# First layer's weight sums converted where they are made, a new product order, other places for raw tokens, and a planner with a DMA queue

## The chip, the cores and the metric

One Trainium2 chip, one of its cores. The metric is device microseconds of one execution, the median of the runs shown. Lower is better.

## The reference

Sigmoid attention for 4 batches of 12 heads, 448 tokens of 64 numbers each, then two feed-forward layers over all 1792 tokens (768 to 2048 to 768):

```python
scores = q @ k.T / sqrt(64) - log(448)          # per batch and head
x = (1 / (1 + exp(-scores))) @ v                # reshaped to 1792 x 768
r = maximum(x @ w_in1, 0);  g = s * r * r + b;  x = g @ w_out1
h = x @ w_in2;  g = maximum(h, 0) + alpha * minimum(h, 0);  y = g @ w_out2
```

The four weight arrays arrive as 64-bit floats; all else is 32-bit.

## The kernel before, in words

**Precision and products.** Each 32-bit operand is split into a high part (a cast on ScalarE) and the rest (a subtraction on VectorE), both in the matmul's fast 32-bit format. `split` does this. A product is then three matmuls (lines 406 to 408): high by low, high by high, low by high. On top of that every layer's matrix product uses one level of a seven-product block scheme, so that a 2 by 2 block product needs the products M1 to M7 instead of eight; the left factors are the weight blocks and their sums (`LEFT`), the right factors are token blocks and their differences.

**Phases.** The tokens are two groups of two batches (g = 0, 1). After attention come eight phases in this order: (layer 0, g 0) in and out, (layer 0, g 1) in and out, then the same two for layer 1. They are numbered 0 to 7 here: even ones are in phases (x times w_in, and the nonlinearity), odd ones out phases (times w_out). Every phase has 504 matmuls of 128 x 128 by 448 columns. An in phase loops over eight block rows (`mp`), each with the seven products in `IN_ORDER` and three 128-deep steps: 63 matmuls. An out phase goes through the seven products in `OUT_ORDER`, each with three block rows of eight steps.

**Weights: quads and units.** `quad` prepares one block row of weights, a "quad" in the code's name. It loads two rows of 64-bit weights into `R64[0]` and `R64[1]`, turns them into 32-bit numbers (line 263 on ScalarE into `CVA`, lines 266 and 271 on VectorE into `QUAD`), makes the four block sums (line 284 on VectorE), and stores the seven blocks to an array in DRAM (`w32`, line 302). A quad has eight VectorE operations. There are 34 quads: 8 for each w_in, 9 for each w_out (three chunks of columns, by three block rows). `QUAD`, `CVA` and `R64` are single, so one quad follows another: the next may write `QUAD` only when the store of the one before has landed. Matmuls get weights by `unit`: it loads 1024 columns from DRAM into one of two `RAW` buffers and splits them into one of three `RING` buffers, 21 units in each phase.

**Tokens.** Seven right factors, the planes `X`, stand in a field of 37 slots (`SLOTS`). `make_x` makes them from four raw token blocks `XRAW` by splits and differences (line 335). For g 0 of layer 0 the raw blocks come straight out of attention, in the memory of the ring. For the other three (layer, group) pairs they are in DRAM, and `load_x` loads them in the out phase before, in its last product, into `XRAW[1]`. This buffer lies on the same memory as `R64`, `CVA` and part of `QUAD` (`PROD`, 5376 columns from its start).

**Order.** Nothing is issued in program order. Every operation is handed to `Plan.add` with an engine, a duration, and the 64-column memory cells that it reads and writes; what touches the same cells keeps program order. `Plan.order` then simulates the engines: at each step it takes the operation that can start first, and among equals the one with the earliest due time; TensorE keeps program order. The due times come from TensorE's ideal times. DMAs are all issued from SyncE's queue, in the order planned; in the plan each holds the queue for its whole transfer. On the chip every engine's operations run in that fixed order and wait for semaphores. `produce(n)` puts the next n quads into the program: 20 during attention (8 w_in1, 9 w_out1, 3 w_in2), 9 after phase 1, 5 after phase 3.

Of the kernel before, what the change touches and what calls it, by code (L numbers as in the profile page):

```python
# [18 lines left out]
CELL = 64  # L19

IN_ORDER = ["M1", "M5", "M6", "M2", "M7", "M4", "M3"]
# [5 lines left out]
class Plan:  # L29
# [25 lines left out]
    def order(self):  # L55
# [5 lines left out]
        ideal, t = {}, 0.0  # L61
        for i, op in enumerate(self.ops):
            if op[0] == "PE":
                ideal[i] = t
                t += op[1]
        late = [0.0] * n
        for i in range(n - 1, -1, -1):
            eng, dur, lat = self.ops[i][:3]
            x = min((late[s] for s in succ[i]), default=t + 50) - dur - lat
            late[i] = min(x, ideal[i]) if i in ideal else x  # L70
        left = [len(op[3]) for op in self.ops]
        est = [0.0] * n
        pe = [i for i in range(n) if i in ideal]
# [5 lines left out]
        free = {}  # L79
        done = []  # L80
        while len(done) < n:
            best = None
            for eng, cand in open_.items():
                if not cand:
                    continue
                f = free.get(eng, 0.0)
                if eng == "PE":
                    i = pe[pe_at]
                    if i not in cand:
                        continue  # L90
                    pick = (max(f, est[i]), late[i], i)
                else:
                    pick = min((max(f, est[i]), late[i], i) for i in cand)
# [7 lines left out]
            end = start + dur  # L101
            free[eng] = end
            done.append(i)
            for s in succ[i]:
                est[s] = max(est[s], end + lat)
# [3 lines left out]
        return done  # L109
# [26 lines left out]
def tile_kernel(  # L136
# [59 lines left out]
    RAW = [own(f"raw{i}", UNIT) for i in range(NRAW)]  # L196
    TMP = [own(f"tmp{i}", S) for i in range(NTMP)]
    NEG = own("neg", 2 * S)
# [7 lines left out]
    def act_t(n, psum=False):  # L206
        return (0.15 if psum else 0.19) + 0.834e-3 * n

    def dve_t(n, psum=False):
        return 0.155 + (1.06e-3 if psum else 1.04e-3) * n  # L210
# [4 lines left out]
    def dma_t(n):  # L215
        return 0.1 + n * 4 * P / 330e3
# [3 lines left out]
    MM = 0.2005  # L220
# [11 lines left out]

    w64 = {(0, "in"): w_in1, (0, "out"): w_out1, (1, "in"): w_in2, (1, "out"): w_out2}
    w32 = {k: drp.tile([P, 7 * NMP * WQ], F32, name=f"w{k[0]}{k[1]}") for k in w64}

    def quad(m, kind, k, c):

        order = IN_ORDER if kind == "in" else OUT_ORDER
# [8 lines left out]
        for row in range(2):  # L247
# [9 lines left out]
            x, y = ("A11", "A12") if row == 0 else ("S3", "A22")  # L257
# [18 lines left out]
            add("ACT", act_t(2 * n), f0, cv, ca)  # L276
# [11 lines left out]
        tt("S1", "S3", "A22", ALU.add)  # L288
        tt("S3", "A11", "S3", ALU.subtract)
# [16 lines left out]
    n_unit = [0]  # L306
    ring = {}

    def unit(m, kind, i):
        g = n_unit[0]  # L310
        n_unit[0] += 1
        raw, dst = RAW[g % NRAW], RING[g % NRING]
        load(
            sb(raw, UNIT), w32[m, kind][:, i * UNIT : (i + 1) * UNIT], UNIT,
            [("d", m, kind, 8 * i + j) for j in range(8)], cells(raw, UNIT),
        )
        split(dst, dst + UNIT, raw, UNIT)
        ring[m, kind, i] = dst
# [27 lines left out]
    X = [[slots(f"xo{p}{i}", p, 3 * i, 3) for i in range(7)] for p in range(2)]  # L346
# [17 lines left out]
    def make_x(par, raw):  # L364
        p = [XRAW[raw] + i * XB for i in range(4)]
        pl = X[par]

        def half(i, src):
            split(pl[i], pl[i] + XB, src, XB)

        half(0, p[0])
        minus(p[0], p[1], p[0], XB)
        half(1, p[0])
        minus(p[0], p[3], p[0], XB)
        half(2, p[0])
        half(3, p[2])
        minus(p[1], p[3], p[1], XB)
        half(4, p[1])
        minus(p[0], p[0], p[2], XB)
        half(5, p[0])  # L380
        half(6, p[3])

    def load_x(m, g):
        for i in (0, 1, 3, 2):
            to = XRAW[1] + i * XB
            load(
                sb(to, XB), x_dram[m, g][:, i * XB : (i + 1) * XB], XB,
                [("x", m, g, i, j) for j in range(KH)], cells(to, XB),
            )
# [51 lines left out]
    def nonlinear(m, par, mp, ps_):  # L441
# [4 lines left out]
        if m == 0:  # L446
# [5 lines left out]
                "ACT", act_t(n) + 0.15,  # L452
# [4 lines left out]
        for row in range(2):  # L457
            some = [p for p in ps_ if p // 2 == row]
            if not some:
# [12 lines left out]
                "DVE", dve_t(n),  # L472
# [6 lines left out]
    def in_phase(m, par):  # L479
        NU = 7 * NMP * KH // 8  # L480
        made = 0
        for mp in range(NMP):
# [3 lines left out]
            second = {"M2", "M4", "M7"}  # L486
            for i, x in enumerate(IN_ORDER):
                terms = []
                for kc in range(KH):
                    g = (mp * 7 + i) * KH + kc  # L490
                    while made <= g // 8:
                        unit(m, "in", made)
                        made += 1
                    w = ring[m, "in", g // 8] + (g % 8) * P
                    xo = X[par][i]
                    terms.append((w, w + UNIT, xo + kc * S, xo + XB + kc * S))
# [18 lines left out]
                elif x == "M4":  # L515
# [3 lines left out]
                else:  # L519
# [20 lines left out]
    def out_phase(m, g, par, middle):  # L540
# [19 lines left out]
        for i, x in enumerate(OUT_ORDER):  # L560
# [4 lines left out]
            for k in range(NDP):  # L565
                unit(m, "out", i * NDP + k)
                w = ring[m, "out", i * NDP + k]
                for (j0, j1), o in zip(CHUNKS, GB[par][i % 2]):
                    terms = [
                        (w + j * P, w + (UNIT + j * P), o + (j - j0) * S, o + (j1 - j0 + j - j0) * S)  # L570
# [79 lines left out]
    def qk(u):  # L650
# [17 lines left out]
        add("PE", 0.81, f, r, pcells(k), PE_LAT)  # L668
# [13 lines left out]
    def av(u):  # L682
# [23 lines left out]
        add("PE", 0.81, f, r + w, w, PE_LAT)  # L706

    def take_x(q):
# [4 lines left out]
        t = XRAW[0] + o if bb < 2 else tmp()  # L713
# [37 lines left out]
    quads = []  # L751
    for m in range(2):
        quads += [(m, "in", k, 0) for k in range(NMP)]
# [92 lines left out]
```

## Time and profile before

| | |
|---|---|
| median of 3 runs | 1026.64 us (1022.49, 1026.64, 1033.18) |
| the profiled execution's own time | 1022.74 us |
| its span, first to last instruction | 1020.9 us |
| mean granted TensorE clock | 0.980 |
| busy: TensorE, weight loads | 972.0 us (95%), 828.7 us (81%) |
| busy: VectorE, ScalarE | 762.6 us (75%), 625.8 us (61%) |
| moved by DMA | 222.68 MB, 218 GB/s over the span |

The span is what the trace covers. The execution's own time is 1.8 us longer, and the median of the runs 3.9 us longer than that. Busy times count an engine's operations; TensorE's matmuls overlap in the pipeline.

### The profile page before, as it was taken

The numbers are of one execution on the slowest core, as the hardware profiler recorded it, in microseconds if no ns is written. First come the engines' busy times: TensorE is split into PE (matmuls) and PEld (weight loads), VectorE is DVE, ScalarE is ACT, GpSimd is POOL, SyncE is SP. The second block draws the span as 40 slices with busy tenths as digits, with TensorE's granted clock in tenths as the row PEclk, the third lists the DMA queues.
The fourth block names the chain that finished last, engine by engine and source line by source line (L and its number), as shares of the span: only waits on it lengthen the run. The fifth ranks groups of instructions, "written<-read, shape, count | busy, mean of one in ns | idle before, by whom it ended". The sixth has DMA issues, their size and how long they took to land.

```text
span 1020.9 us, 13856 instructions
## 1 busy us (share of the span) xinstructions
PE 972.0 (95%) x5424; PEld 828.7 (81%) x5424; DVE 762.6 (75%) x896; ACT 625.8 (61%) x675; POOL 0.2 (0%) x4
## 2 busy tenths in 40 slices
PE   9999999998699979999999889998999999999998
PEld 5533368987598968999899769997999999999997
DVE  2476467679996867668999589868997856679872
ACT  7889856877553536778665246656645455576440
POOL 0000000000000000000000000000000000000000
PEclk9999999998899999999999989998999999999999
DMA  8998999886776657776579568765444533333441
GB/s 302 332 336 300 354 330 353 281 286 193 275 258 223 208 185 285 239 253 222 166 241 313 198 233 281 226 216 200 116 122 147 163 111 111 104 106 105 146 138 67
DMA packets 70625, 222.68 MB, mean 218 GB/s; under 512 B 6688, under 2 KB 30624, under 8 KB 68512
## 3 DMA queue, kind: packets, MB, share of 16 engines
q1 hardware_dynamic: 70560, 221.81, 64.6%
q8 instruction: 42, 0.69, 0.3%
q14 instruction: 23, 0.19, 0.0%
HBM read 163.98 MB, written 57.80 MB: 217 GB/s over the span
## 4 chain that ended last, share of the span: by engine, by line
PE 62%; DVE 11%; DMA 6%; ACT 3%; issue 3%; SPq 0%; DVEq 0%; ACTq 0%
PE ps L406 21%; PE ps L408 21%; PE ps L407 21%; DMA xraw<-x 3%; DVE ring L325 2%; DVE xo L325 2%; DVE gb L325 1%; DVE g L335 1%; DVE quad L284 1%; DMA r<-in_w_in 1%; DVE xraw L335 1%; DVE tmp L427 1%; ACT gb L322 1%; DVE quad L271 1%; DMA raw<-w0in 1%
## 5 line engine op out<-in xcount | busy, mean ns | idle before, releaser
L406 PE MATMUL ps<-xo,ring 128*128 128x448 f32 x672 | 250.9, 373 | 22.3 <-DVE tmp L427 18.7
L322 ACT CAST ring<-raw 128x1024 fp32r<-128x1024 f32 x168 | 175.3, 1047 | 154.6 <-PE ps L407 111.9
L406 PE MATMUL ps<-gb,ring 128*128 128x448 f32 x672 | 249.1, 371 | 10.7 <-ACT ring L322 7.5
L408 PE MATMUL ps<-gb,ring 128*128 128x448 f32 x672 | 249.0, 371 | 9.4 <-DVE ring L325 9.4
L407 PE MATMUL ps<-xo,ring 128*128 128x448 f32 x672 | 249.0, 370 | 0.0
L408 PE MATMUL ps<-xo,ring 128*128 128x448 f32 x672 | 248.7, 370 | 0.0
L407 PE MATMUL ps<-gb,ring 128*128 128x448 f32 x672 | 248.1, 369 | 0.0
L325 DVE TENSOR_TENSOR ring<-raw,ring 128x1024 fp32r<-128x1024 f32 x168 | 204.2, 1217 | 24.7 <-ACT ring L322 24.6
L406 PEld LDWEIGHTS ps<-xo,ring 128*128 128x128 f32 x672 | 128.6, 191 | 39.3 <-DVE tmp L427 23.1
L406 PEld LDWEIGHTS ps<-gb,ring 128*128 128x128 f32 x672 | 128.2, 191 | 23.4 <-ACT ring L322 10.6
L408 PEld LDWEIGHTS ps<-gb,ring 128*128 128x128 f32 x672 | 128.0, 190 | 22.1 <-DVE ring L325 11.5
L408 PEld LDWEIGHTS ps<-xo,ring 128*128 128x128 f32 x672 | 128.5, 191 | 10.7
L407 PEld LDWEIGHTS ps<-xo,ring 128*128 128x128 f32 x672 | 128.5, 191 | 10.3
L407 PEld LDWEIGHTS ps<-gb,ring 128*128 128x128 f32 x672 | 128.3, 191 | 10.4
L427 DVE TENSOR_TENSOR tmp<-ps,tmp 128x448 f32<-128x448 f32 x124 | 76.7, 619 | 71.0 <-PE ps L408 58.2
L325 DVE TENSOR_TENSOR gb<-g,gb 128x1344 fp32r<-128x1344 f32 (+1 forms) x84 | 116.1, 1395 | 10.1 <-ACT gb L322 7.7
L322 ACT CAST gb<-g 128x1344 fp32r<-128x1344 f32 (+1 forms) x84 | 99.3, 1190 | 21.2 <-PE ps L408 14.5
L677 ACT ACTIVATE sg<-ps,bias 128x896 f32<-128x896 f32 x84 | 82.9, 1009 | 13.3 <-PE ps L661 12.6
L263 ACT ACTIVATE cva<-r 128x768 f32<-128x768 f32 (+1 forms) x68 | 59.0, 868 | 51.5 <-DVE quad L271 20.0
L271 DVE SCALAR_TENSOR_TENSOR quad<-cva,quad 128x768 uint32<-128x768 uint32 (+1 forms) x68 | 61.5, 905 | 30.6 <-DMA xraw<-x 18.5
L661 PE MATMUL ps<-kq 64*64 64x448 f32 x672 | 80.9, 542 | 2.0 <-ACT sg L677 2.0
L699 PE MATMUL ps<-sg,v 64*64 64x448 f32 x672 | 80.0, 536 | 0.0
(32 smaller groups left out, 656.8 us busy)
## 6 DMA issues: line engine op xcount, KB each, us to landing
r<-in_w_in SPq DMA_DIRECT2D x32, 768.0 KB, 5.4
raw<-w0in SPq DMA_DIRECT2D x42, 512.0 KB, 4.5
raw<-w0out SPq DMA_DIRECT2D x42, 512.0 KB, 4.3
raw<-w1in SPq DMA_DIRECT2D x42, 512.0 KB, 3.7
raw<-w1out SPq DMA_DIRECT2D x42, 512.0 KB, 3.5
r<-in_w_out SPq DMA_DIRECT2D x24, 768.0 KB, 5.9
w0in<-quad SPq DMA_DIRECT2D x8, 1344.0 KB, 7.5
w1in<-quad SPq DMA_DIRECT2D x8, 1344.0 KB, 5.3
```

The source lines that it names most:

```text
L263: nc.scalar.activation(a, hi, AF.Prelu, scale=2.0**-112, alpha=-(2.0**32))
L271: nc.vector.scalar_tensor_tensor(out=u, in0=a.bitcast(U32), scalar=3, in1=u, op0=ALU.logical_shift_left, op1=ALU.bitwise_or,)
L322: add("ACT", act_t(n), lambda: nc.scalar.copy(h, x), cells(src, n), cells(hi, n))
L325: lambda: nc.vector.tensor_tensor(out=l, in0=x, in1=h.bitcast(F32), op=ALU.subtract),
L335: lambda: nc.vector.tensor_tensor(out=o_, in0=x_, in1=y_, op=ALU.subtract),
L406: nc.tensor.matmul(d, wh_, ml_, start=first and k == 0, stop=False, **opt)
L407: nc.tensor.matmul(d, wh_, mh_, start=False, stop=False, **opt)
L408: nc.tensor.matmul(d, wl_, mh_, start=False, stop=last and k == n, **opt)
L427: lambda: nc.vector.tensor_tensor(out=d, in0=bank(k), in1=o, op=ALU.add),
L661: nc.tensor.matmul(ps[h * D : (h + 1) * D, k + j, :S], a.ap[rows, S + k0 : S + k0 + D], a.ap[rows, :S], start=True, stop=True,)
L677: lambda: nc.scalar.activation(o, i, AF.Sigmoid, bias=sb(BIAS, 1), scale=QKSCALE),
L699: nc.tensor.matmul(ps[j * D : (j + 1) * D, k + h, :S], va[keys, v : v + D], a.ap[keys, j * S : (j + 1) * S], start=first, stop=last,)
```

## The change

For the first in phase (layer 0, g 0) the weights no longer go to DRAM and back: `direct` splits the seven blocks of a quad straight out of the buffer where it was made, two blocks at a time, into a ring of four entries (`RING4`, the same memory as the three `RING` buffers). There are two such quad buffers now: `QUAD` in its old place and a second one in `SPARE`, memory that it shares with the two `RAW` buffers and with `NEG`. Quads of w_in1 alternate between them and are made just ahead of use: two in attention, and after each block row the quad for the row after the next. They are still stored to DRAM, for g 1. Seven quads of w_out1 are made in attention, between the two of w_in1, the last two in the middle of phase 0. All 17 quads of layer 1 follow phase 0 in the program. One temporary moves (`S1` holds the raw block that `S3` held), and M4 now precedes M7 in `IN_ORDER`; the accumulator updates for both follow M7. The raw tokens from DRAM go to five small tensors in slots 16 to 21, which are free in every out phase, and in `NEG`; two of the planes `X` for one parity change places for it, and one raw block is in two pieces, so that its operations are two each. In the planner a DMA holds SyncE's queue for 0.07 us only, and a model of the shared transfer pipe (335 GB/s) may run 1 us ahead; due times are made three times, each from the starts found by the pass before; durations are set a little anew. `MORE` is empty, so that `whl` and `save` do nothing.

```diff
-IN_ORDER = ["M1", "M5", "M6", "M2", "M7", "M4", "M3"]
+QUEUES = {"SP": 0.07, "POOL": 1.0}
+AHEAD = 1.0
+ROUNDS = 3
+EARLY = 7
+MORE = []
+IN_ORDER = ["M1", "M5", "M6", "M2", "M4", "M7", "M3"]
...
+        for _ in range(ROUNDS):
+            late = [0.0] * n
+            for i in range(n - 1, -1, -1):
+                dur, lat = self.ops[i][1:3]
+                x = min((late[s] for s in succ[i]), default=t + 50) - dur - lat
+                late[i] = min(x, goal[i]) if i in goal else x
+            done, at = self.place(succ, late, list(goal))
+            goal = {i: at[i] for i in goal}
+        return done
...
+                if eng in QUEUES:
+                    f = max(f, pipe - AHEAD)
...
+            if eng in QUEUES:
+                free[eng] = start + QUEUES[eng]
+                pipe = max(pipe, start) + dur
+                end = pipe
+            else:
+                end = free[eng] = start + dur
...
+    SPARE = take(NRAW * UNIT + 2 * S)
     RING = [tensor(f"ring{i}", RING0 + i * 2 * UNIT, 2 * UNIT, F32R) for i in range(NRING)]
-    XRAW = {0: tensor("xraw0", RING0, 4 * XB), 1: tensor("xraw1", PROD, 4 * XB)}
+    RING4 = [tensor(f"rinq{i}", RING0 + i * 4 * WQ, 4 * WQ, F32R) for i in range(4)]
+    RAW = [tensor(f"raw{i}", SPARE + i * UNIT, UNIT) for i in range(NRAW)]
+    NEG = tensor("neg", SPARE + NRAW * UNIT, 2 * S)
+    MID = SLOTS + 16 * SLOT
+    XRAW[1] = [
+        [(tensor("xraw10", MID + 2 * SLOT, XB), 0, XB)],
+        [(tensor("xraw11", MID, XB), 0, XB)],
+        [(tensor("xraw12", MID + 2 * SLOT + XB, XB), 0, XB)],
+        [(tensor("xraw13", MID + XB, S), 0, S), (tensor("xraw14", NEG.base, 2 * S), S, XB)],
+    ]
-    QUAD = tensor("quad", PROD + 10 * WQ, 7 * WQ)
+    QUADS = [tensor("quad", PROD + 10 * WQ, 7 * WQ), tensor("quadb", SPARE, 7 * WQ)]
...
-        tt("S1", "S3", "A22", ALU.add)
-        tt("S3", "A11", "S3", ALU.subtract)
+        tt("S3", "A11", "S1", ALU.subtract)
+        tt("S1", "S1", "A22", ALU.add)
...
+    def direct(mp, place):
+
+        for b0, b1 in ((0, 2), (2, 4), (4, 6), (6, 7)):
+            n = (b1 - b0) * WQ
+            dst = entry((7 * mp + b0) * WQ, n, RING4)
+            split(dst, dst + n, QUADS[place] + b0 * WQ, n)
+            yield
...
-    X = [[slots(f"xo{p}{i}", p, 3 * i, 3) for i in range(7)] for p in range(2)]
+    X = [
+        [slots(f"xo{p}{i}", 0, k, 3) for i, k in enumerate(ks)]
+        for p, ks in enumerate(([0, 3, 6, 9, 12, 18, 15], [34, 31, 28, 25, 22, 19, 16]))
+    ]
...
-        minus(p[1], p[3], p[1], XB)
-        half(4, p[1])
-        minus(p[0], p[0], p[2], XB)
-        half(5, p[0])
+        less(p[0], p[0], p[2])
+        half(4, p[0])
+        less(p[1], p[3], p[1])
+        half(5, p[1])
...
+            if m == g == 0:
+                get = direct(mp, 1 - mp % 2)
...
+                    while (m or g) and made <= n // 8:
+                        unit(m, "in", made, g)
                         made += 1
+                    if m == g == 0 and i % 2 == 0 and kc == 0:
+                        next(get)
...
+            if m == 0 and g == 0 and mp + 2 < NMP:
+                if mp % 2 == 1 and EARLY + mp // 2 < len(outs):
+                    quad(*outs[EARLY + mp // 2])
+                quad(m, "in", mp + 2, 0, 1 - mp % 2)
...
+    quads = [(0, "in", 0, 0, 1)]
+    outs = [(0, "out", k, c) for c in range(len(CHUNKS)) for k in range(NDP)]
+    quads += outs[:EARLY]
+    quads += [(0, "in", 1, 0, 0)]
+    quads += [(1, "in", k, 0) for k in range(NMP)]
+    quads += [(1, "out", k, c) for c in range(len(CHUNKS)) for k in range(NDP)]
...
-            produce(20)
+            produce(2 + EARLY)
...
+        in_phase(m, g, par)
+        if n == 0:
+            produce(len(quads))
...
-        if n == 0:
-            produce(9)
-        if n == 1:
-            produce(len(quads))
```

## Rows read from the trace of the kernel before

**Rows 1.** Busy time by stretch: attention, then phases 0 to 5 (cut at matmuls).

```profile
core 0: us, PE busy (x) PEld busy (x) DVE busy (x) ACT busy (x) POOL busy (x), PEclk, DMA share, GB/s
0.00:134.00 134.00, 130.96 (x1392) 61.24 (x1392) 71.09 (x101) 115.02 (x134) 0.20 (x4) 1.00 0.90 323
134.00:248.10 114.10, 105.74 (x509) 95.55 (x505) 85.70 (x125) 81.05 (x82) 0.00 (x0) 0.98 0.86 296
248.10:369.40 121.30, 110.15 (x505) 98.54 (x506) 102.56 (x110) 61.25 (x65) 0.00 (x0) 0.93 0.66 226
369.40:481.70 112.30, 104.75 (x505) 95.61 (x504) 79.06 (x107) 77.71 (x75) 0.00 (x0) 0.98 0.74 254
481.70:591.70 110.00, 104.51 (x505) 95.71 (x505) 95.00 (x102) 59.25 (x63) 0.00 (x0) 0.98 0.69 227
591.70:710.20 118.50, 108.87 (x506) 98.46 (x505) 97.81 (x129) 70.02 (x84) 0.00 (x0) 0.94 0.70 236
710.20:812.40 102.20, 102.20 (x506) 94.64 (x506) 90.30 (x80) 56.89 (x57) 0.00 (x0) 1.00 0.43 131
```

**Rows 2.** The same view, of blocks of 72 or 144 matmuls around phase borders.

```profile
229.90:277.40 47.50, 34.59 (x146) 29.62 (x145) 44.05 (x57) 31.55 (x37) 0.00 (x0) 0.86 0.69 228
321.20:339.70 18.50, 16.79 (x74) 14.66 (x73) 13.08 (x15) 5.80 (x7) 0.00 (x0) 0.91 0.83 299
369.40:393.80 24.40, 16.93 (x73) 14.56 (x72) 15.35 (x21) 9.66 (x11) 0.00 (x0) 0.93 0.80 291
481.70:498.50 16.80, 14.85 (x73) 13.44 (x73) 16.80 (x16) 15.54 (x19) 0.00 (x0) 1.00 0.35 100
571.50:614.60 43.10, 34.66 (x146) 30.02 (x145) 33.29 (x35) 17.99 (x18) 0.00 (x0) 0.88 0.64 225
687.70:710.20 22.50, 17.76 (x74) 15.57 (x73) 18.85 (x24) 11.51 (x14) 0.00 (x0) 0.85 0.65 223
```

**Rows 3.** Chain that ended last, 305 to 345 us: start, duration, what.

```profile
311.76 5.35 DMA xraw<-x
...
317.20 0.10 DVE quad L271
...
320.72 3.91 DMA xraw<-x
```

**Rows 4.** VectorE's waits, 134 to 710 us: total, times, longest.

```profile
DVE quad L271 <- DMA xraw<-x: 18.5, 4, 5.5
...
DVE quad L284 <- DMA xraw<-x: 6.3, 2, 4.0
DVE quad L266 <- DMA w0out<-quad: 5.2, 3, 3.0
DVE quad L271 <- ACT cva L263: 4.5, 6, 1.0
```

**Rows 5.** Timeline of SyncE's queue around the border of phases 0 and 1.

```profile
253.63 0.34 SPq L229 DMA_DIRECT2D raw<-w0out  x1
...
262.04 0.53 SPq L302 DMA_DIRECT2D w0out<-quad  x1
```

**Rows 6.** DMA issues: count, KB each, median us from issue to landing.

```profile
r<-in_w_in SPq DMA_DIRECT2D x32, 768.0 KB, 5.4
raw<-w0in SPq DMA_DIRECT2D x42, 512.0 KB, 4.5
...
w0in<-quad SPq DMA_DIRECT2D x8, 1344.0 KB, 7.5
```

**Rows 7.** Busy time of VectorE on quads, and its operations, by stretch.

```profile
0.00:134.00 134.00, 39.73 (x64) 1.00 0.90 323
134.00:248.10 114.10, 35.33 (x61) 0.98 0.86 296
...
369.40:481.70 112.30, 25.14 (x40) 0.98 0.74 254
...
sum 1017.40, DVE 160.38; mean DVE 17.82
```

More of the change, by code (lines that the diff above doesn't have):

```diff
@@ L78, in order @@
                 open_.setdefault(self.ops[i][0], set()).add(i)
-        free = {}
-        done = []
+        free, done, at = {}, [], {}
+        pipe = 0.0
         while len(done) < n:
@@ L304, in quad, with saved, entry, unit @@
         )
-    n_unit = [0]
+    whl = {k: drp.tile([P, 2 * 7 * NMP * WQ], F32R, name=f"s{k[0]}{k[1]}") for k in SAVED}
+    n_unit = [0, 0]
     ring = {}
-    def unit(m, kind, i):
-        g = n_unit[0]
+    def saved(m, kind, at, n):
+        return whl[m, kind][:, 2 * at : 2 * (at + n)], [("h", m, kind, at)]
+    def entry(at, n, ring_=RING):
+        dst = ring_[n_unit[0] % len(ring_)]
         n_unit[0] += 1
-        raw, dst = RAW[g % NRAW], RING[g % NRING]
+        for j in range(n // P):
+            ring[at // P + j] = (dst + j * P, dst + (n + j * P))
+        return dst
+    def unit(m, kind, i, g):
+        at, n = i * UNIT, UNIT
+        dst = entry(at, n)
+        if (m, kind) in SAVED and g == 1:
+            src, there = saved(m, kind, at, n)
+            load(sb(dst, 2 * n), src, 2 * n, there, cells(dst, 2 * n))
+            return
+        raw = RAW[n_unit[1] % NRAW]
+        n_unit[1] += 1
         load(
-            sb(raw, UNIT), w32[m, kind][:, i * UNIT : (i + 1) * UNIT], UNIT,
-            [("d", m, kind, 8 * i + j) for j in range(8)], cells(raw, UNIT),
-        )
-        split(dst, dst + UNIT, raw, UNIT)
-        ring[m, kind, i] = dst
+            sb(raw, n), w32[m, kind][:, at : at + n], n,
+            [("d", m, kind, 8 * i + j) for j in range(8)], cells(raw, n),
+        )
+        split(dst, dst + n, raw, n)
+        save(m, kind, at, n, dst)
+    def save(m, kind, at, n, dst):
+        if (m, kind) in SAVED:
+            d, there = saved(m, kind, at, n)
+            x = sb(dst, 2 * n)
+            add(
+                "SP", dma_t(2 * n), lambda: nc.sync.dma_start(out=d, in_=x),
+                cells(dst, 2 * n), there, DMA_LAT,
+            )
+    def direct(mp, place):
[4 more added lines that the diff above has]
+            yield
     def split(hi, lo, src, n):
@@ L384, in load_x @@
         for i in (0, 1, 3, 2):
[L385 to L389, printed above, removed]
+            for to, a, e in XRAW[1][i]:
+                load(
+                    sb(to, e - a), x_dram[m, g][:, i * XB + a : i * XB + e], e - a,
+                    [("x", m, g, i, j) for j in range(a // S, e // S)], cells(to, e - a),
+                )
     def bank(k):
@@ L750, in tile_kernel @@
     )
-    quads = []
-    for m in range(2):
-        quads += [(m, "in", k, 0) for k in range(NMP)]
-        quads += [(m, "out", k, c) for c in range(len(CHUNKS)) for k in range(NDP)]
+    quads = [(0, "in", 0, 0, 1)]
[4 more added lines that the diff above has]
+    quads += [(1, "out", k, c) for c in range(len(CHUNKS)) for k in range(NDP)]
     def produce(n):
```

84 lines of the change are left out of this document (40 added, 44 removed).

## The prediction

> **What bounds the kernel now.** I read the table of busy times by stretch first, cut where one phase's first matmul begins [rows 1]. Phase 5 is the yardstick: TensorE is busy for all of its 102.2 us at full clock, which is 0.2028 us for each of 504 matmuls; phases 6 and 7 are as long within half a microsecond. That is the floor for this arithmetic, and the last three phases sit on it. Phases 0 to 4 do the same matmuls in 114.1, 121.3, 112.3, 110.0 and 118.5 us. Over 102.2 each they lose 11.9, 19.1, 10.1, 7.8 and 16.3, together 65.2 us of a span of 1020.9. Attention shows no such loss (131 of 134 us busy). So all that can be won lies in phases 0 to 4, and the only work that these have and the last three have not is quads.
>
> The same view in smaller blocks says where [rows 2]. 72 matmuls take 14.6 us at the floor. The border of phases 0 and 1 (229.9 to 277.4) takes 47.5 us for two blocks, 29.2 at the floor: **18.3** lost. The border 1 to 2 loses 3.9 before and 9.8 behind it, **13.7**; the border 2 to 3 **2.2**; the border 3 to 4 43.1 - 29.2 = **13.9**; the end of phase 4 **7.9**. What is left of phase 0 before 229.9 is 95.9 us for six blocks and the start, 87.6 at the floor: **8.3**. These make 64.3; some tenths elsewhere make up the rest. A part is not idleness: in those blocks the granted clock averages 0.85 to 0.93 [rows 2], so some of the matmuls behind a gap run at the lower level, 1.2 GHz. A gap costs more than its length, and a gap removed gives both back.
>
> Then the reasons, from the chain and the waits. In the chain before the border 1 to 2 a load of raw tokens and the quads release each other in turn [rows 3]: the load issued at 311.76 lands at 317.11 and a quad operation starts at 317.20; the next token load is issued at 320.72, when a quad is done with its buffers. The quad operation of line 271 doesn't use the columns of that block; the two share `PROD`, and the wait follows the shared tensor. In phases 0 to 4 VectorE stood 18.5 + 6.3 = 24.8 us before quad operations that a token load released, six times [rows 4]. The borders 1 to 2, 3 to 4 and the end of phase 4 show the same pair. The border 0 to 1 has another reason: the last quad of w_out1 is stored at 262.04, 14 us after the phase that needs it began, and loads of its units go out only behind those stores [rows 5].
>
> **The change, part by part.**
>
> *Token loads away from `PROD`.* No quad touches slots 16 to 21 or `NEG` after phase 0, and in an out phase no plane lives there. The loads can go out as soon as the in phase ends, 100 us before use. What is late next is VectorE itself: an out phase with its token work and without quads takes 90.3 of 102.2 us, as in phase 5 [rows 1], and there it loses nothing. So a border costs what phase 5's does, 0, plus what quads bring. A quad takes VectorE 160.38 / 34 = 4.72 us [rows 7]; other waits at quads were 5.2 + 4.5 = 9.7 us for some 26 quads behind attention [rows 4], 0.4 each; with full VectorE such a wait is not caught up. I take 4 us for each of the two borders (bounds 0 and today's 13.9), and 1 us for the end of phase 4, where by count the quads should be over: 13.7 + 13.9 + 7.9 = 35.5 becomes 9. **Gain 26.5 us.** The three or four more VectorE operations for the raw block in two pieces fall in the 11.9 us free; without that cover they would be 4 x 0.59 = 2.4 (0.59 being a mean quad operation, 160.38 / 272).
>
> *w_out1 earlier.* Seven of its nine quads are made in attention, the other two by the fourth block row of phase 0. Today attention makes eight quads and phase 0 some 7.6 (64 and 61 operations, eight a quad) [rows 7]; that is enough for nine and eight in the new order, and the last one of w_out1 is about fifth of those. It is then ready before 200 at 10 us a quad, by 224 at today's 15.0, and phase 1 starts at 236 or later. The border 0 to 1 should cost what the border 2 to 3 costs, where the weights were ready: 18.3 becomes 2.2. **Gain 16.1 us** (bounds: 0 if the quads stay as late, 18.3).
>
> *Direct splits.* They drop 21 loads of 512 KB [rows 6], 11 MB, and the way of these weights over DRAM. ScalarE and VectorE convert the same columns in 32 pieces instead of 21 units. Eleven more operations each are at most 11 x 0.59 = 6.5 us, in a phase in which VectorE is idle for 114.1 - 85.7 = 28 [rows 1]: nothing. But quads of w_in1 now stand on TensorE's path. The second is the ninth quad; at attention's pace of 134 / 8 = 16.8 us [rows 7] it would be done at 151, and some 3 MB that no longer go before it (about four units and a third of a quad) give back 3 MB / 323 GB/s = 10 us: 141, against 146.8 when block row 1 starts. From there eight quads must be arithmetic-complete by the start of block row 7, 134 + 7 x 12.8 = 223: 10 us each. Today phase 0 makes one in 15.0 us [rows 7], because the next must wait until the store has landed, 7.5 us [rows 6], behind some 7 us of arithmetic. With two buffers, five of the eight are in the one and three in the other: 5 x 14.5 from 141 is 214, in time. Bytes allow it: 8 x 2.95 MB at 323 GB/s [rows 6, 1] is 73 us of 82. I leave phase 0's 8.3 us as it is; bounds 0, and 37 if the pace stays 15.0 (141 + 120 + 12.8 = 274 against the floor's 236).
>
> In the stretch that moves most, the transfers run at 323 GB/s with their engines 0.90 busy [rows 1], and by that rate eight quads need 73 us. The Trainium skill (Perfetto Trace Analysis, Roofline) lets a single core draw more than its HBM share, up to about 435 GB/s of its 16 DMA engines. By that rule the eight would need 54 us, an estimate from that page, bytes would bind nowhere in phase 0, its term could fall to its lower bound of 0, and the sum to 974. A full share would be 323 / 0.90 = 359 GB/s here, so the trace does not agree, and the rows decide.
>
> *Product order.* M7's and M4's accumulator updates both follow M7, one matmul group before M3 as now; bank `c` is next written two block rows later. Nothing.
>
> *The planner.* Other due times, and DMAs that queue instead of holding SyncE. Every engine's order is new. No row prices that; it is inside the bounds above, and a rival below. Waits added: `RAW`'s first loads for phase 1 now wait for the last splits out of the second quad buffer (block row 6), with one block row, 12.8 us, to land in 4.5 [rows 6]; only other unit loads stand behind them on SyncE.
>
> **Sum.** 1022.74 (the profiled execution) - 26.5 - 16.1 = 980.1. The median of the runs lay 3.9 above that execution; half of this, 2, I carry over: **982 us**.
>
> **Rivals.**
>
> *Quads crowd phase 1.* Nothing holds the 17 quads of layer 1 back now. At phase 0's 15.0 us a quad, seven would enter phase 1 [rows 7]; VectorE has room for 11.9 / 4.72 = 2.5. The other 4.5 would cost 21 us: 1003. For it: VectorE was already busy for 102.6 us there, more than the floor is long [rows 1]. Against: none of them is due for 200 us, and the planner prefers what is due first; and phase 2, with 33 us free and five quads, lost time at its border only.
>
> *The first in phase waits for its quads* (the slower side). It is decided by the pace of quads in phase 0. If a quad takes p, the phase ends at 141 + 8p + 12.8. The gain of 42.6 is used up at p = 16.7; at phase 2's pace, five quads in 112.3 us or 22.5 [rows 7], it ends at 334 instead of 244.5, 89 us later: about 1071. For it: today's 15.0 is not far from that point. Against: both of today's paces hold a store's landing in series, and nobody waited for phase 2's quads.
>
> *It doesn't do what it says.* Waits follow whole tensors, and `quadb` now shares memory with `RAW` and `NEG`; the planner's times may be off in other places than before. If as much is lost anew as is removed, 1017 to 1037.
>
> **How the numbers follow.** Forecast (966 to 995): 0.62. Crowding or a phase 0 at today's pace (995 to 1015): 0.18. No net change: 0.11. Slower by the second rival: 0.09. The range takes in all terms at their better bounds (980 - 8 - 9 = 963, so 962) and above the crowded case, 1012; about 0.2 stays outside. A change of 1% (10 us, the runs spread over 10.7) is what this measurement can tell from none: faster 0.81, same 0.11, slower 0.08.
>
> **What would show it.** Right: phases 1 and 3 near 106 us, no quad operation released by a token load, the last store of w_out1 before 200, a mean clock of 0.99. Wrong: gaps of TensorE in phase 0 that a direct split releases (the second rival), or VectorE full in phase 1 with more than five quads in it (the first).

## The result, and the profile after

The changed kernel takes **994.23 us** (median of 4 runs, 988.16 to 999.66) against 1024.87 us before (4 runs, 1022.49 to 1033.18): a ratio of 0.9685 [0.9604, 0.9767], faster by 31 us. It lies 12 us above the predicted 982 and inside the range of 962 to 1012. The profiled execution is the slowest of the four, 999.66 us with a span of 997.9.

First the busy times by stretch, cut as in [rows 1]: attention, then phases 0 to 7.

```profile
core 0: us, PE busy (x) PEld busy (x) DVE busy (x) ACT busy (x) POOL busy (x), PEclk, DMA share, GB/s
0.00:135.10 135.10, 132.19 (x1393) 53.45 (x1393) 72.93 (x104) 115.53 (x138) 0.20 (x4) 1.00 0.92 326
135.10:239.40 104.30, 102.68 (x509) 94.49 (x505) 93.06 (x147) 78.58 (x87) 0.00 (x0) 1.00 0.73 265
239.40:345.90 106.50, 104.73 (x505) 94.56 (x506) 97.64 (x95) 66.52 (x70) 0.00 (x0) 1.00 0.63 208
345.90:450.00 104.10, 104.10 (x505) 94.57 (x504) 77.10 (x103) 76.04 (x73) 0.00 (x0) 1.00 0.74 248
450.00:554.20 104.20, 104.20 (x506) 94.64 (x505) 96.07 (x93) 62.10 (x64) 0.00 (x0) 1.00 0.56 183
554.20:659.20 105.00, 104.33 (x505) 94.43 (x504) 93.26 (x130) 67.45 (x81) 0.00 (x0) 1.00 0.82 288
659.20:785.70 126.50, 109.03 (x504) 96.52 (x505) 103.84 (x100) 60.87 (x63) 0.00 (x0) 0.95 0.48 152
785.70:889.90 104.20, 104.20 (x506) 94.64 (x505) 66.39 (x79) 57.73 (x70) 0.00 (x0) 1.00 0.36 108
889.90:994.50 104.60, 104.58 (x505) 94.34 (x503) 75.22 (x70) 46.30 (x48) 0.00 (x0) 1.00 0.37 115
```

Read the first column of lengths against [rows 1]. Phases 0 to 4 gave back 9.8, 14.8, 8.2, 5.8 and 13.5, together 52.1 us. Phase 5, the old yardstick, lost 24.3 (126.5 against 102.2). Attention lost 1.1, and phases 6 and 7 together 3.8 (208.8 against 205.0). The sum, 22.9 us, is the difference of the two last matmuls (1017.4 in [rows 7], 994.5 here), and of the spans it is 23.0.

Two things in the table were not forecast. One is phase 5. The other is harder to see: phases 3 and 6 are **busy for all of 104.2 us**, at a granted clock of 1.00, while the same 504 matmuls took 102.2 before. More on this under the experiments.

The same view of the first 72 matmuls behind the borders 0 to 1, 1 to 2, 3 to 4 and 4 to 5:

```profile
239.40:256.60 17.20, 15.43 (x72) 13.46 (x73) 17.20 (x16) 16.65 (x19) 0.00 (x0) 1.00 0.70 235
345.90:360.80 14.90, 14.90 (x74) 13.54 (x73) 12.44 (x18) 6.54 (x8) 0.00 (x0) 1.00 0.84 294
554.20:569.10 14.90, 14.90 (x74) 13.53 (x73) 10.52 (x15) 5.03 (x6) 0.00 (x0) 1.00 0.83 295
659.20:696.50 37.30, 19.83 (x73) 15.48 (x74) 33.32 (x37) 16.38 (x20) 0.00 (x0) 0.82 0.56 189
```

The blocks behind 1 to 2 and 3 to 4 have no idle time at all, where [rows 2] had 24.4 us and the second half of 43.1. Behind 0 to 1 there remain 2.6 us over the floor of 14.6, with VectorE busy for the whole block; 1.8 of them are idle time of TensorE. Behind 4 to 5 a block takes 37.3 us. What was waited for is in TensorE's waits (engine, line, waited for; total us, times, longest):

```profile
PE ps L480 <- ACT ring L386: 15.1, 3, 7.0
PE ps L480 <- DVE gb L389: 4.4, 4, 2.1
```

All but 1.1 of the 15.1 us lie in phase 5: two gaps of 7.0. SyncE's queue around them (start, us, line, what):

```profile
646.39 0.53 SPq L332 DMA_DIRECT2D w1out<-quad  x1
...
661.49 0.53 SPq L332 DMA_DIRECT2D w1out<-quad  x1
670.71 6.13 SPq L257 DMA_DIRECT2D raw<-w1out  x2
677.32 0.53 SPq L332 DMA_DIRECT2D w1out<-quad  x1
```

And the matmuls that end them (idle before, releaser, in brackets):

```profile
675.29 0.74 PE L480 MATMUL ps<-gb,ring 128*128 128x448 f32 x1 [6.98 <-ACT ring L386]
...
689.57 0.74 PE L480 MATMUL ps<-gb,ring 128*128 128x448 f32 x1 [7.00 <-ACT ring L386]
```

It is the pattern that [rows 5] showed at the border 0 to 1, now in the other layer. The last two quads of w_out2 are stored at 661.49 and 677.32, both behind the start of phase 5 at 659.20. Units of them can be loaded only then, split on ScalarE, and multiplied: TensorE goes on 13.8 and 12.3 us behind the two stores. A matmul directly behind a gap takes 0.57 to 0.74 us instead of 0.37; the block's mean clock is 0.82, so part of it ran at 1.2 GHz. The two gaps are 14.0 of the 22.4 us that the block loses against its 14.9. Shorter idle times make up another 3.5 (37.3 less 19.8 busy, less 14.0), and the slower matmuls the last 4.9 (19.8 busy instead of 14.9).

Why so late? Busy time of VectorE on the buffer `quad` and its operations, attention and phases 0 to 5 (the view of [rows 7]). Quads made in `quadb` are not in it, and phase 0's row holds 16 operations of direct splits out of `quad`; from phase 1 on it counts every quad, at eight operations each:

```profile
0.00:135.10 135.10, 35.09 (x56) 1.00 0.92 326
135.10:239.40 104.30, 43.54 (x67) 1.00 0.73 265
239.40:345.90 106.50, 8.96 (x14) 1.00 0.63 208
345.90:450.00 104.10, 25.37 (x39) 1.00 0.74 248
450.00:554.20 104.20, 7.14 (x11) 1.00 0.56 183
554.20:659.20 105.00, 35.55 (x58) 1.00 0.82 288
659.20:785.70 126.50, 5.10 (x11) 0.95 0.48 152
```

Phase 1 makes under two quads and phase 3 about one and a half; VectorE is busy there for 97.6 and 96.1 us in all. Phase 2 makes five, with 27 us of VectorE left free. Between 440.59 and 543.82, for 103 us, no quad is stored. Of the rest 58 operations are squeezed into phase 4, at about one quad in 15 us (the stores at 646.39, 661.49 and 677.32), and 11 spill over into phase 5.

### The profile page after: what moved, and what is told of

It reads as the page before. It is cut to its first block, busy times and chain, and to the rows that moved or that the text cites. A ratio compares the mean times of both kernels' runs of the same rounds, so it can differ in the third digit from the quotient of the medians.

```text
span 997.9 us, 13846 instructions
## 1 busy us (share of the span) xinstructions
PE 970.0 (97%) x5424; PEld 811.7 (81%) x5424; DVE 776.1 (78%) x916; ACT 631.1 (63%) x689; POOL 0.2 (0%) x4
## 4 chain that ended last, share of the span: by engine, by line
PE 86%; DMA 7%; DVE 4%; ACT 2%; issue 1%; ACTq 0%; DVEq 0%; SPq 0%
PE ps L480 27%; PE ps L482 27%; PE ps L481 27%; DMA w0out<-quad 3%; PE ps L740 3%; PE ps L778 2%; DMA w1out<-quad 1%; DMA r<-in_w_out 1%; DVE quad L314 1%; ACT sg L756 1%; DMA raw<-w1out 1%; DVE quad L301 1%; DVE ring L389 0%; ACT cva L293 0%; DVE gb L389 0%
## 5 line engine op out<-in xcount | busy, mean ns | idle before, releaser
L480 PE MATMUL ps<-gb,ring 128*128 128x448 f32 x672 | 249.5, 371 | 19.6 <-ACT ring L386 15.1
L386 ACT CAST ring<-raw 128x1024 fp32r<-128x1024 f32 x147 | 153.8, 1047 | 158.9 <-PE ps L481 133.4
L389 DVE TENSOR_TENSOR ring<-raw,ring 128x1024 fp32r<-128x1024 f32 x147 | 179.3, 1220 | 28.1 <-ACT ring L386 27.7
L480 PE MATMUL ps<-xo,ring 128*128 128x448 f32 x504 | 185.5, 368 | 0.0
L481 PE MATMUL ps<-xo,ring 128*128 128x448 f32 x504 | 185.5, 368 | 0.0
L482 PE MATMUL ps<-xo,ring 128*128 128x448 f32 x504 | 185.5, 368 | 0.0
L386 ACT CAST gb<-g 128x1344 fp32r<-128x1344 f32 (+1 forms) x84 | 99.8, 1192 | 28.0 <-PE ps L482 23.1
L481 PEld LDWEIGHTS ps<-xo,ring 128*128 128x128 f32 x504 | 94.6, 188 | 9.6
L482 PEld LDWEIGHTS ps<-xo,ring 128*128 128x128 f32 x504 | 94.6, 188 | 9.5
L480 PEld LDWEIGHTS ps<-xo,ring 128*128 128x128 f32 x504 | 94.6, 188 | 9.5
L756 ACT ACTIVATE sg<-ps,bias 128x896 f32<-128x896 f32 x84 | 83.2, 1010 | 12.1 <-PE ps L740 11.3
L778 PE MATMUL ps<-sg,v 64*64 64x448 f32 x672 | 77.9, 536 | 0.0
L399 DVE TENSOR_TENSOR g<-g 128x1344 f32<-128x1344 f32 (+1 forms) x48 | 66.3, 1396 | 2.6 <-ACT xo L386 2.5
```

The source lines that it names most:

```text
L386: add("ACT", act_t(n), lambda: nc.scalar.copy(h, x), cells(src, n), cells(hi, n))
L389: lambda: nc.vector.tensor_tensor(out=l, in0=x, in1=h.bitcast(F32), op=ALU.subtract),
L399: lambda: nc.vector.tensor_tensor(out=o_, in0=x_, in1=y_, op=ALU.subtract),
L480: nc.tensor.matmul(d, wh_, ml_, start=first and k == 0, stop=False, **opt)
L481: nc.tensor.matmul(d, wh_, mh_, start=False, stop=False, **opt)
L482: nc.tensor.matmul(d, wl_, mh_, start=False, stop=last and k == n, **opt)
```

## The experiments

The theory after the result: **the change does at the borders what it says; what it lost, it lost because layer 1's quads were placed too late to be ready for phase 5, and because this one execution's matmuls ran at a slower pace.** Rivals: the pace belongs to the new program; the planner alone made the gain; the late quads are a matter of room on the engines, not of placement.

**The same kernel once more.** No edit.

> The changed kernel itself once more, for its stretches without a stall. In its first trace 72 matmuls take 14.6 us up to 223 us and 14.9 us in all stretches from 257 us on, with no gap and at full clock; in the trace of before nearly all take 14.6. Theory A: the pace is drawn anew at every stall of TensorE, not set by the program: this trace has the same stalls (22 us at the start of phase 5, about 4 us at the border of phases 0 and 1), but at least one of the long stretches between them at another pace than in the first trace, and the times spread over 10 us or more (985 to 1000). Theory B: the program's addresses or order set the pace: again 14.9 from phase 1 to the end, and a time near 1000.

991.3 us (988.01 to 991.66), 0.9679 [0.9642, 0.9716]. Phases 2 and 3 of the profiled execution, whose span is 986.2:

```profile
346.60:448.70 102.10, 102.10 (x505) 94.65 (x504) 77.34 (x103) 75.61 (x73) 0.00 (x0) 1.00 0.72 254
448.70:550.90 102.20, 102.20 (x506) 94.72 (x506) 95.77 (x93) 62.17 (x65) 0.00 (x0) 1.00 0.54 188
```

The same program on the same data: 102.2 us for what took 104.2 above, both without a gap and at full clock. So the program doesn't set the pace; it differs from one execution to the next. The rest of theory A did not come: the four times spread over 3.7 us, not 10, and this trace has the stalls but keeps the faster pace through all of them. The stall of phase 5 is there again (124.0 us). The trace of before ran at the faster pace but for short stretches, so stage by stage this execution, 988.01 us, is the nearer one to compare the terms of the sum with; the 982 itself was a forecast of the median, which was 994.23 there and is 991.3 here.

**Tokens back into `PROD`.**

```diff
-    MID = SLOTS + 16 * SLOT
-    XRAW[1] = [
-        [(tensor("xraw10", MID + 2 * SLOT, XB), 0, XB)],
...
-    ]
+    XRAW_ = tensor("xraw1", PROD, 4 * XB)
+    XRAW[1] = [[(XRAW_ + i * XB, 0, XB)] for i in range(4)]
```

> The raw tokens are loaded to PROD again, everything else as changed. My theory: the loads of raw tokens and the quads wait for each other because they share that memory; so quad operations released by token loads come back (about 25 us of VectorE's waiting before), gaps return behind the ends of phases 1, 3 and 4, and the time rises by 15 to 30 us over the changed kernel, to 1010 to 1022. Rival: in the new order of quads (two in phase 1, one in phase 3) there is no quad left to collide with at these borders: less than 8 us, under 1002. Second rival: the quads are held back so far by token loads that the stall in phase 5 grows by 20 us or more: over 1022.

1104.9 us, 1.0794 [1.0744, 1.0843]. **No theory had this:** the time is in the second rival's range, but the stall is in phase 1, and phase 5 takes 104.2 us, without a stall. Phase 1, TensorE's longest wait, and SyncE's queue near its end:

```profile
240.30:471.80 231.50, 107.58 (x504) 96.81 (x505) 156.30 (x205) 83.86 (x92) 0.00 (x0) 0.73 0.75 265
```
```profile
PE ps L475 <- DVE xo L384: 125.2, 3, 120.9
```
```profile
457.50 5.78 SPq L252 DMA_DIRECT2D xraw<-x  x2
468.78 0.53 SPq L327 DMA_DIRECT2D w1out<-quad  x1
472.86 0.80 SPq L252 DMA_DIRECT2D xraw<-x  x2
```

TensorE stood for 120.9 us. Operations on the same memory keep program order, and all 17 quads of layer 1 now stand ahead of phase 1's token load in the program. With tokens in `PROD` that load had to wait for every one of them: two blocks, which lie on `R64`, go out at 457.50, when the last quad has read it; the other two, which reach into `QUAD`, only at 472.86, behind the last store of all at 468.78. So the test doesn't isolate the mutual waits. It shows that the two halves of the change are no separate terms: `produce` may put all quads behind phase 0 only because the tokens have left their memory. Tokens back with the quads placed as before was not tried in this form; the next run comes from the other side.

**Only the tokens moved.** The kernel before, with raw tokens in slots 16 to 21 and `NEG`, and the product order and plane places that this needs; quads, planner and `produce` as before.

```diff
-IN_ORDER = ["M1", "M5", "M6", "M2", "M7", "M4", "M3"]
+IN_ORDER = ["M1", "M5", "M6", "M2", "M4", "M7", "M3"]
-    XRAW = {0: tensor("xraw0", RING0, 4 * XB), 1: tensor("xraw1", PROD, 4 * XB)}
+    XRAW[1] = [
+        [(tensor("xraw10", MID + 2 * SLOT, XB), 0, XB)],
...
+    ]
```

> The kernel before with one part of the change: raw tokens in slots 16 to 21 and NEG, and with it the product order and the planes' places that this needs; old planner, old order of quads, no direct splits. My theory: it takes away the losses at the borders 1 to 2, 3 to 4 and at the end of phase 4 (13.7 + 13.9 + 7.9 us) but for some 9 us, and leaves the 18 us at the border 0 to 1 and the 8 us in phase 0: 26 us less than before, near 998. Rival: these borders are lost because VectorE is full there with quads and tokens at once, whatever the memory: 1015 or more.

1005.68 us, 0.9811 [0.9777, 0.9846]. Phases 0 to 4:

```profile
133.10:258.50 125.40, 104.72 (x509) 95.75 (x505) 97.17 (x135) 89.29 (x91) 0.00 (x0) 0.94 0.81 285
258.50:380.10 121.60, 110.17 (x505) 99.59 (x506) 101.24 (x117) 60.59 (x62) 0.00 (x0) 0.92 0.73 257
380.10:482.30 102.20, 102.20 (x506) 94.62 (x505) 79.09 (x107) 75.76 (x74) 0.00 (x0) 1.00 0.75 268
482.30:588.70 106.40, 103.89 (x505) 95.84 (x504) 100.36 (x102) 63.67 (x67) 0.00 (x0) 0.98 0.60 203
588.70:693.00 104.30, 104.30 (x505) 94.45 (x505) 84.82 (x117) 63.67 (x78) 0.00 (x0) 1.00 0.65 222
```

Phases 2 to 4 take 312.9 us instead of 340.8 [rows 1]: 27.9 gained, beside a forecast of 26.5 for this part. Phase 0 is 11.3 us longer, phase 1 0.3. The plan, made anew, stored the last quad of w_out1 at 273 instead of 262 [rows 5], so the border 0 to 1 cost more: some 36 us instead of 18. That side effect, 11.6 us in phases 0 and 1, is more than the 7.7 us that the total lacks against the 998 expected. No quad operation of this run waits for a token load, so the rival, a full VectorE whatever the memory, falls for the borders 1 to 2 and 3 to 4.

**Only the planner.** The kernel before with the new `Plan`, durations and `QUEUES`, `AHEAD` and `ROUNDS`; tokens, quads and product order as before.

```diff
+QUEUES = {"SP": 0.07, "POOL": 1.0}
+AHEAD = 1.0
+ROUNDS = 3
...
+                if eng in QUEUES:
+                    f = max(f, pipe - AHEAD)
```

> The kernel before with the new planner alone (DMA queue model, three passes, new durations). Theory A: the planner brings none of the gain, for token loads and quads still share PROD and w_out1's quads are still last: within 10 us of before (1013 to 1033), with the same stalls around the phase borders. Theory B: three passes give due times that follow the stalls, so what is late gets later, as in the changed kernel's phase 5: slower than before by over 10 us. Theory C: the queue model keeps transfers from colliding and is part of the gain: faster by over 10 us.

1030.73 us over 10 runs, 1.0051 [1.0028, 1.0075]: alone it brings nothing, as theory A had it. VectorE still stands before quads that token loads release (22.0 us in all; the worst group 12.4 us, three times). The half per cent need not be the planner's: the profiled execution has phases 1 to 3 and 7 at the slower pace, about 8 us.

**w_out1 late again.** Three of its quads in attention, three in the middle of phase 0, three behind w_in1's last.

```diff
-EARLY = 7
+EARLY = 3
-                if mp % 2 == 1 and EARLY + mp // 2 < len(outs):
+                if mp % 2 == 1:
+            quads[:0] = outs[EARLY + 3 :]
```

> The changed kernel with w_out1's quads later: three in attention (seven as changed), three in the middle of phase 0 and the last three behind the last w_in1 quad. My theory: the border of phases 0 and 1 was lost in the kernel before because these quads were stored only in phase 1 (the last at 262 us); stored late again, they bring back a stall of 10 to 25 us at the start of phase 1, whose end releases are loads of w0out and ring conversions: 1000 to 1016. Rival: the border was lost to VectorE's load (differences and splits of the next phase), which is as it was: under 996.

998.06 us, 0.9736 [0.9691, 0.978]. Phases 0 and 1:

```profile
133.00:249.50 116.50, 105.62 (x509) 96.24 (x505) 96.79 (x151) 84.45 (x93) 0.00 (x0) 0.95 0.67 244
249.50:370.20 120.70, 109.67 (x505) 99.16 (x506) 108.16 (x114) 66.17 (x70) 0.00 (x0) 0.93 0.69 239
```

237.2 us, as long as before the change (235.4 [rows 1]); 210.8 after it. The place of these quads is worth 26 us there, and TensorE's longest waits there are for ring conversions (15.6 us in three gaps), as expected. The total is in neither range, over the rival's 996 and under the theory's 1000: it cost only 4 to 7, because the quads of layer 1 were planned otherwise and phase 5 took 110.0 us instead of 126.5 (124.0 in the second execution). A term can be right in its stage and not show in the total.

**First layer's weights over DRAM again,** in the new quad order: no direct split, one quad buffer.

```diff
-            if m == g == 0:
-                get = direct(mp, 1 - mp % 2)
...
-                    while (m or g) and made <= n // 8:
+                    while made <= n // 8:
...
-                quad(m, "in", mp + 2, 0, 1 - mp % 2)
+                quad(m, "in", mp + 2, 0)
...
-    quads = [(0, "in", 0, 0, 1)]
+    quads = [(0, "in", 0, 0, 0)]
```

> The changed kernel, its order of quads kept, but without direct splits: phase 0 takes its weights over DRAM again, and all quads use one buffer. My theory: with one buffer a quad waits for the store of the one before (some 7 us of arithmetic and 7 us of store), so eight quads after the second w_in1 quad (146 us) take 8 x 14.5 us, and store, load and conversion add about 12 us before the last block row can start: phase 0 ends near 146 + 116 + 12 + 13 = 287 us instead of 240, with TensorE waiting for ring conversions in many block rows; phases 1 to 7 as in the changed kernel: 1030 to 1045. Rival: the pace of 15 us was only that of quads that nobody waited for; hurried, they come every 10 us: phase 0 longer by 10 to 15 us, 1000 to 1008.

1021.15 us over 10 runs, 0.9963 [0.9937, 0.9989]. Phase 0, and TensorE's waits in the whole run:

```profile
137.00:273.90 136.90, 113.00 (x509) 99.91 (x506) 95.98 (x140) 80.68 (x80) 0.00 (x0) 0.90 0.78 289
```
```profile
PE ps L480 <- ACT ring L386: 33.0, 6, 10.3
```

Phase 0 is 32.6 us longer than with direct splits; of the 33.0 us of waits 20.6 are in it, the rest at the start of phase 5, which stalls as before. The total lies between the theory's range and the rival's. Quad stores follow each other by 13.1 us (eight intervals from 142 to 247), not the 14.5 that I took for a single buffer, so the phase ends at 274 rather than at about 287. Nearly the whole gain of the change is gone: making w_in1 just ahead of use, which is what sets w_out1 free, pays only if the quads come at the pace that two buffers and no way over DRAM allow. Which of these two carries it was not tried.

**One pass of due times.** Three passes set due times from the starts found by the pass before. The theory: a quad that came late in one pass is allowed to be late in the next.

```diff
-ROUNDS = 3
+ROUNDS = 1
```

> The changed kernel with one pass of due times (ROUNDS = 1) in place of three; the due times are then counted back from TensorE's gapless starts, not from the starts of a plan that already has the stall in it. Theory A: the quads of w_out2 end 17 us after phase 5 begins because repeated passes move their due times back by the stall that they cause: with one pass the last store of a quad is near 665 us instead of 677, and the stall at the start of phase 5 (22 us) shrinks to 12 or less: 10 to 15 us faster, near 982. Theory B: there is no room for them, because one quad buffer gives one quad per 15 us and VectorE is full in phases 1 and 3: the same stall, within 4 us.

973.22 us, 0.9491 [0.9449, 0.9532]: 18 us faster than the changed kernel's 991.3, measured alongside it. The last store and phase 5:

```profile
656.27 0.53 SPq L332 DMA_DIRECT2D w1out<-quad  x1
```
```profile
656.00:764.90 108.90, 105.05 (x505) 95.56 (x505) 98.04 (x90) 58.55 (x60) 0.00 (x0) 0.98 0.49 163
```

The planner's own figures (computed with the changed kernel's code, `Plan.order`; they are in no trace) show how. For the store of the last quad its due time is 645.4 us in the first pass, 663.1 in the second and 669.2 in the third, and the starts that the passes plan are 661.8, 668.6 and 673.7: each pass takes over the lateness of the one before. Even the first plans it 16 us late, so one pass mends this only in part.

**Layer 1's quads due sooner,** with three passes: 120 us for w_in2, 30 us for w_out2.

```diff
+HURRY = {"in": 120.0, "out": 30.0}
...
+        self.sooner[i] = self.hurry
...
+            late = [x - self.sooner[i] for i, x in enumerate(late)]
...
+            plan.hurry = HURRY[quads[0][1]] if quads[0][0] else 0.0
```

> The changed kernel, three passes kept, but in the planner the due times of layer 1's quads lie earlier: 120 us for the w_in2 quads, 30 us for the w_out2 quads. If three passes hurt only because they let those quads slip (theory A of the run with one pass), this mends it too: last store of a quad before 655 us, no stall of TensorE over 3 us at the start of phase 5, and a time within 6 us of the one-pass kernel's 973. Rival: the passes harm other things as well (an order that follows stalls everywhere): the stall in phase 5 goes, but the time stays over 982.

971.34 us, 0.9469 [0.9433, 0.9504]. The last store is at 628.20, and phase 5 has one gap of 3.4 us, just over the 3 expected. VectorE's operations on quads in phases 2 to 4:

```profile
345.80:447.90 102.10, 32.52 (x50) 1.00 0.80 292
447.90:550.10 102.20, 13.11 (x20) 1.00 0.64 218
550.10:653.60 103.50, 27.60 (x49) 1.00 0.72 253
```

Phase 2 takes 50 operations instead of 39 and phase 3 20 instead of 11, both without a loss. There was room for these quads all along, in the out phase too; only the planner's due times kept them out of it. Two rivals fall: too little room on the engines, and that the passes harm other things as well.

In this trace the slower pace begins at 584 us and holds to 885. It begins with no pause of TensorE at all.

**One pass without the queue model.**

```diff
-QUEUES = {"SP": 0.07, "POOL": 1.0}
+QUEUES = {}
...
-ROUNDS = 3
+ROUNDS = 1
```

> The one-pass kernel without the DMA queue model: a DMA holds SyncE's queue in the plan for its whole transfer, as before the change. If the model does little (theory A), the time is within 5 us of the one-pass kernel's 973. If letting SyncE run ahead by 1 us of the pipe is what keeps quads fed (theory B), quads come later and phase 5's stall grows: 980 or more.

983.65 us, 0.9614 [0.9567, 0.9662], 10 us behind the 973.22 with it. The planner's DMA queue does help in the new arrangement; in the old one the new planner as a whole brought nothing. Theory B has the time, and its cause only in part: the last quad is stored at 660 instead of 656, and phases 4 and 5 take 108.4 and 111.0, together 4.6 us more. Attention is 3 us longer, but it differs by as much between two executions of the changed kernel (135.1 and 138.2). Where the rest comes from is open.

**Both: one pass, and quads due sooner** (130 and 30 us).

```diff
-ROUNDS = 3
+ROUNDS = 1
+HURRY = {"in": 130.0, "out": 30.0}
```

> One pass and earlier due times for layer 1's quads (130 and 30 us). In the one-pass kernel phases 4 and 5 still take 105.9 and 108.9 us against 102.1, with the last quad stored at 656 us, when phase 5 begins. With the quads some 10 to 20 us earlier both phases should come to 104 or less: 5 to 9 us under the one-pass kernel, 964 to 968, the fastest of all. Rival: earlier quads take VectorE's time from phases 1 to 3, which have none to spare: gaps return there, and the time is 973 or more.

**967.88 us** over 6 runs, 0.9436 [0.9407, 0.9465]: faster than the kernel before and the changed one. Its interval overlaps those of the two runs that it combines. The last store, then phases 4 and 5:

```profile
625.48 0.52 SPq L336 DMA_DIRECT2D w1out<-quad  x1
```
```profile
551.80:654.20 102.40, 102.40 (x506) 94.52 (x505) 92.86 (x127) 66.52 (x83) 0.00 (x0) 1.00 0.71 244
654.20:756.30 102.10, 102.10 (x506) 94.61 (x505) 92.74 (x85) 57.30 (x59) 0.00 (x0) 1.00 0.47 160
```

With the last store 29 us ahead of phase 5 both phases are at the floor, and no gap of more than 1.1 us is left in TensorE's waits. The rival has a small part: phase 2 takes 105.3 us, 3.2 more than with one pass alone.

## Why the prediction was nearly right, point by point

| part | forecast gain, us | in the profiled execution | in the second one |
|---|---|---|---|
| attention | 0 | -1.1 | -4.2 |
| phases 0 and 1 | 16.1 | 24.6 | 27.0 |
| phases 2 to 4 | 26.5 | 27.5 | 33.4 |
| phase 5 | 0 | -24.3 | -21.8 |
| phases 6 and 7 | 0 | -3.8 | 0.2 |
| sum | 42.6 | 22.9 | 34.6 |

Each is the length in [rows 1] (205.0 for phases 6 and 7 of before) less the length after; the second execution's phases 0 to 7 are 103.8, 104.6, 102.1, 102.2, 103.1, 124.0, 102.1 and 102.7, behind 138.2 of attention. The border 1 to 2, part of the forecast 26.5, has 3.9 of its 13.7 us in phase 1, so some 3 of the 26.5 belong in the row above. Attention is the same work in both executions after; it varied by 3.1 us between them.

**How near, and how much of it luck.** The median came 12 us over the 982 (9 in the second set of runs), but as a sum of errors: phase 5 lost 22 to 24 us that stood in no term, and phases 0 to 4 gained 9.5 (17.8) more than forecast, which happened to hide much of it.

- **Token loads away from `PROD`: right, and under-sized.** I left 4 us at each of two borders, for waits at quads; they came to nothing. No quad operation in phases 0 to 4 waits for a token load, where [rows 4] had 24.8 us. The run with this part alone gained 27.9.
- **w_out1 earlier: right.** The last store was forecast before 200 and came at 185; the border keeps 3.9 us (1.3 at the end of phase 0, 2.6 behind it) where I forecast 2.2.
- **Direct splits: right in mechanism.** The second quad of w_in1, whose arithmetic was forecast to end at 141, was stored at 145, the eighth, forecast for 214, at 223. With w_out1's two in between, that is eight quads in 78.3 us or 9.8 each; the 10 that were needed were there, and barely. Phase 0's 8.3 us, which I kept whole, fell to 0.8 (the phase is 2.1 over the floor, 1.3 of that already counted at the border). The lower bound was the nearer one. (The 3 MB at 323 GB/s are 9.3 us, not the 10 of the sum; nothing hangs on it.) Splits and second buffer were not tried apart.
- **The step that failed: that by the end of phase 4 "by count the quads should be over", and with it no term at all for phase 5.** The 1 us itself held: the last 72 matmuls of phase 4 take 1.1 us over the floor (1.0 in the second execution). The quads were not over; the last two were stored behind the start of phase 5, whose first 72 matmuls lost 22.4 us. I looked for the danger on the crowding side, seven quads in phase 1; the reverse happened, under two each in phases 1 and 3. The count was sound: my 2.5 quads for an out phase are the 20 operations that phase 3 took without loss once they were due sooner. What it lacked was a reason why the planner should use the room in time. The cause is the planner's due times. Phase 5 lost 22.3 and 21.8 us over its pace's floor in the two executions with three passes, 6.7 with one pass, 5.2 with three passes and earlier due times, and nothing with both.
- **The planner "inside the bounds above":** it wasn't, and this is why the step above failed. By itself it brings nothing (1.0051); in the new arrangement its queue is worth 10 us, and its repeated passes cost 18.
- **The rivals.** Crowding of phase 1 didn't come, nor did the wait for w_in1's quads, though the run over DRAM shows how near it is: at 13.1 us a quad phase 0 already takes 32.6 us more. That the change doesn't do what it says is refuted by phases 0 to 4. All signs of being right came too: phases 1 and 3 at 106.5 and 104.2 us, no quad operation released by a token load, the last store of w_out1 at 185, a mean clock of 0.993. None of these signs looked at phase 5.
- **Pace.** My sum had 42.6 us less, the profiled execution 23.1. Of the 19.5 between them 11.7 vanish in the second execution of the same program: phases 0 to 7 are 14.8 shorter there, nearly all of it pace, and attention is 3.1 longer. The trace of before holds the slower pace too, the longest time from 332 to 365 us, but in stretches too short to show in a phase.

The transfers of attention run at 326 GB/s with their engines 0.92 busy, a full share of 354; in the trace before, 150 to 180 us have a share of 1.00 and move 360 GB/s. No stretch here comes near the 435 GB/s that the Trainium skill allows a single core (Perfetto Trace Analysis, Roofline), so the rows were the right side to decide by. Phase 0's term did fall almost to its lower bound, but at 265 GB/s and a share of 0.73, so not by that rule.

## What to carry to other kernels

When a change lets work move freely between stages, count for each stage how much of it that stage's engines can take, and then ask what makes the planner use that room, and by when the last piece must be there. Room that nothing obliges the planner to use stays empty: here 103 us passed without one quad stored. Due times that are made again from the schedule they produced make every lateness legal: in this kernel one pass was better than three. And two edits that touch the same memory are one edit: tokens out of the quads' buffers and all quads early in the program belong together. The whole change was 31 us faster than the kernel before, and the same change without the tokens' move 82 us slower.

## What the runs showed of the hardware

Matmuls of 128 x 128 by 448 columns, each with new weights, ran at **two steady paces at full clock**: 14.6 us for 72 (202.7 ns from start to start) and 14.9 us (206.7 ns). Phases 2, 3 and 6 of the first trace after have no idle time and take 104.1 to 104.2 us; the second execution of the same program takes 102.1 to 102.2. A matmul in the slower stretches lasts 368 ns on average, in the faster ones 365. In the first trace the change of pace came where TensorE had paused (around 246 us). It doesn't need a pause: in the run with layer 1's quads due sooner it came at 584 us, amid matmuls without any idle time. The pace accounts for some 14 us between the two spans, of which a longer attention takes back 3. What draws it is open. Whoever compares two traces should first compare a phase without idle time. For matmuls back to back at 2.4 GHz the Trainium skill gives a start-to-start time of N / 2.4 GHz and about 2.5 ns (TensorE: Matmul & The Clock Gate, "Wait — 56ns, not 53.3ns?"), by estimate from that page 189 ns for 448 columns. The traces here don't agree: no stretch of these matmuls, with a weight load for each, averages under 202 ns.
